# One PSUM ring for first scores and transposes, an earlier order of first scores, and sums and norms on GpSimd

## The chip, the cores and the metric

The kernel runs on one core of a Trainium2 chip. The metric is the device time of one execution in microseconds (us); lower is better. The engines of the core run side by side, each through its own list of instructions in order: TensorE (PE, with its weight loads PEld), VectorE (DVE), ScalarE (ACT), GpSimd (POOL) and SyncE (SP), which issues all DMAs of this kernel. TensorE writes its products to PSUM, here eight banks of 128 partitions by 512 fp32.

## The reference

A transformer block over 2048 rows of width 448, with an adaptive layer norm, sliding attention of 16 heads (28 wide, window 256) and a feed-forward part of width 1792:

```python
mod = (_silu(c) @ w_mod).reshape(c.shape[0], 6, 1, -1)
sa, ca, ga, sb, cb, gb = (mod[:, 0], mod[:, 1], mod[:, 2], mod[:, 3], mod[:, 4], mod[:, 5])
h = _layernorm(x, axis=-1) * (1 + ca) + sa
x = x + ga * _A_ref(h, A_wqkv, A_wo)      # softmax(q k^T, masked to the last 256 keys) v, then wo
h = _layernorm(x, axis=-1) * (1 + cb) + sb
x = x + gb * _B_ref(h, B_w1, B_b1, B_w2)  # mish(h w1 + b1) w2
return x
```

## The kernel before

The rows are cut into four groups of 512. Matrices are held as a rounded part and a rest (the tiles with h and l in their names), and a product is made of up to three passes, so that little accuracy is lost.

**Stages.** A prologue loads, makes the first two modulation vectors and the first group's q, k and v. Then comes the attention stage, the loop `for u in range(NU + 7)`, with NU = 192 units. After it, the feed-forward stage, which the change leaves alone.

**Heads, quads and units.** There are 64 heads i (16 in each of four groups, NS = 64). Four heads are a quad Q, and a quad has 12 units: unit u = 12 Q + 4 b + a is block b of head 4 Q + a. What one unit issues on TensorE is written out by hand in the loop.

- `A(i, t)` makes *first scores* for rows t of head i: one product of 384 columns into a bank of the tag sA (L687), and the rows' maximum by VectorE (L689). When a pair of heads is through, `M1` puts its eight maxima into a small tile `ms` (two VectorE steps).
- `M2(pr)` transposes the maxima of the pair pr on TensorE (L705), copies them by VectorE (L707) and writes them by a DMA into two more rows of the pair's q tiles. So the second scores come out with the maximum taken off.
- `B(u)` makes *second scores* in a bank sB0 or sB1 (L731; masks by TensorE, L759, or laid in by ScalarE, L739) and takes their exponential by ScalarE (L734).
- `PV(w)` multiplies four heads' exponentials with v (L769), `EV(q)` copies a quad's result to SBUF, `E(q)` transposes it on TensorE (L780), and `E2(q)` divides by the sums on VectorE (L788, L790).
- `L(i)`, called by `load_slot`, loads q and k of head i from DRAM into one of eight slots each. A slot is free when the second scores of head i - 8 have been made.

**Banks.** Before, the eight banks are sA two, mm two, sB0, sB1, pv and tr one each. `bank(tag, bufs, name)` takes the next of a tag's banks in a ring, and what writes it waits until the readers of its last content are through. The maxima's transposes and the outputs' transposes use tr.

**The order around the change.** In unit r of a quad (r = u mod 12), the first scores of the *next* quad stand at r = 1 to 10: score n (of 16) in unit 1 + 10 n // 16, the first of a unit right behind `B`, a second one at the unit's end; in unit 3 the first stands behind the filling work. `M2` stands at r = 7 and 11, the loads of a quad's four heads at units 8, 11, 14 and 16 counted from two quads before, and `E` and `E2` at r = 3 and 4 of the second quad behind.

**Filling work.** Between these, generators put other work in small steps: `fill_main` (transposes of the normed rows, q, k, v, the output product), taken by a credit of RATE per unit, and `side` (norms `gen_ln1`, weighted sums `gen_wm_sum`, weights), one step per unit. A step that yields "dve" is put off when the unit has two first scores. DMAs that a step needs later wait in the list `later`, from which the loop takes one in some of the units.

**Weighted sums and norms.** `gen_wm_sum(i)` loads four pieces of 112 rows of w_mod's column block i and adds them up, each scaled by a column of sT, with `mod_sum` (L167 for the first piece, L169 for the other three). It runs four times in the attention stage (i = 2, 3, 4, 5). Its result goes into a product on TensorE: L577 for i = 2, L174 for 3 and 4, L873 for 5. `gen_ln` norms four tiles of rows; L244 is the subtraction and scaling. It is used with the pool qk for the groups 2 and 3 before the attention of these groups, and with other pools later.

Of the kernel before, what the change touches and what calls it, by code (L numbers as in the profile page):

```python
# [12 lines left out]
ALU = mybir.AluOpType  # L13
# [38 lines left out]
def adaln_block(ctx: ExitStack, tc: tile.TileContext, x, wqkv, wo, w1, b1, w2, c, w_mod, out):  # L52
# [112 lines left out]
    def mod_sum(k, w, acc):  # L165
        if k == 0:
            DVE.tensor_scalar(acc, w, sT[:, 0:1], None, op0=ALU.mult)  # L167
        else:
            DVE.scalar_tensor_tensor(acc, w, sT[:, k:k + 1], acc, op0=ALU.mult, op1=ALU.add)  # L169
# [50 lines left out]
    def gen_ln(tiles, pl, xn_tiles, key, act=False, mv=None):  # L220
        if mv is None:
            mv = pl.tile([128, 4, 2], F32, name=f"mv{key}", tag="mv", bufs=2)
            for t in range(4):
                ln_stats(tiles[t], mv[:, t, :], pl, f"{key}{t}")
                if t < 3:
                    yield
        rs = pl.tile([128, 4], F32, name=f"rs{key}", tag="rs", bufs=2)
        POOL.tensor_scalar(rs, mv[:, :, 1], EPS, None, op0=ALU.add)
        POOL.tensor_tensor(rs, rs, mhalf, op=ALU.pow)
        yield  # L230
        if act:
            nm = pl.tile([128, 4], F32, name=f"nm{key}")
            POOL.tensor_tensor(nm, mv[:, :, 0], rs, op=ALU.mult)
            POOL.tensor_scalar(nm, nm, -1.0, None, op0=ALU.mult)
        yield
        xs = xn_tiles()
        for t in range(4):
            xn = xs[t]
            if act:
                ACT.activation(xn[:, 0:D], tiles[t], AF.Identity, scale=rs[:, t:t + 1], bias=nm[:, t:t + 1])  # L240
                dup(xn)
                yield xs
                continue
            DVE.tensor_scalar(xn[:, 0:D], tiles[t], mv[:, t, 0:1], rs[:, t:t + 1],  # L244
                              op0=ALU.subtract, op1=ALU.mult)
            if t:
                dup(xs[t - 1])
            yield xs
        if not act:
            dup(xs[3])  # L250
# [220 lines left out]
    pm = [bank("sA", 2, f"mc{h}") for h in range(2)]  # L471
# [28 lines left out]
    first = [(m, bank(tag, b, f"qk0_{m}"), qk_passes(0, m)) for m, tag, b in ((0, "pv", 1), (3, "tr", 1), (4, "sA", 2))]  # L500
# [72 lines left out]
    def gen_mod_wo():  # L573
        acc = yield from gen_wm_sum(2, qk)
        yield "bank"
        p = bank("mm", 2, "ga")
# [20 lines left out]
    def gen_mod_ln2(i):  # L597
        acc = yield from gen_wm_sum(i, qk)
        yield "bank"
        p = bank("mm", 2, f"mc{i}")  # L600
# [79 lines left out]
    def A(i, t):  # L680
# [5 lines left out]
        p = bank("mm" if i >= 60 and t % 2 else "sA", 2, f"sA{i}_{t}")  # L686
# [16 lines left out]
    def M2(pr):  # L703
        p = bank("tr", 1, f"mt{pr}")
# [72 lines left out]
    def E(q):  # L777
        p = bank("tr", 1, f"et{q}")
# [62 lines left out]
    def gen_w1():  # L841
# [19 lines left out]
        p = bank("mm", 2, "b1t")  # L861
# [10 lines left out]
        pb = bank("mm", 2, "gb")  # L872
# [235 lines left out]
    credit = 0.0  # L1108
    for u in range(NU + 7):
# [11 lines left out]
        q, r = divmod(u, 12)  # L1121
        if u < NU:
            B(u)
        tiles = [divmod(n, 4) for n in range(16) if 1 + n * 10 // 16 == r and 4 * q + 4 < NS]
        if r != 3:
            for a, t in tiles[:1]:
                A(4 * q + 4 + a, t)
        if r in (7, 11) and 4 * q + 4 < NS:
            M2(2 * q + 2 + (r == 11))
        for a in range(4):  # L1130
            if (u - (8, 11, 14, 16)[a]) % 12 == 0 and u >= (8, 11, 14, 16)[a]:
                load_slot(4 * ((u - (8, 11, 14, 16)[a]) // 12) + 8 + a)
        if r - 3 in (0, 1) and 0 <= (u - 12 - 3) // 12 < NS // 4:
            (E, E2)[r - 3](q - 1)
        if g < NG:
# [8 lines left out]
            if r == 3:  # L1144
                for a, t in tiles[:1]:
                    A(4 * q + 4 + a, t)
            if v > 1 and u > 10:
                side_step(g, len(tiles) > 1)
            if later and r in (1, 4, 5, 6, 8, 9) and u not in (4, 11, 12):
# [8 lines left out]
        for a, t in tiles[1:]:  # L1158
            A(4 * q + 4 + a, t)
# [98 lines left out]
```

## Time and profile before

| | us |
|---|---|
| median of 3 runs | 678.75 |
| lowest and highest | 676.63, 680.4 |
| span of the profiled execution | 674.8 |
| distance of the median from that span | 3.95 |

The profile is of one execution. A row of a group reads: line, engine, operation, out<-in, shape, xcount, then busy time and mean ns of one, then the idle time of the engine just ahead of them and what ended it. A row of a wait reads: who waited, at which line, for whom; total us, times, longest. A row of the timeline reads: start, length, engine, line, operation, and in brackets the idle time ahead of it. L59 is the helper that issues every DMA, so SP's rows are told apart by their tiles: q<-scr and k<-scr are the loads of `L`, q<-mr the maxima's rows of `M2`. PE's matmuls overlap, so the lengths shown for them add up to more than their starts allow.

### The profile page before, as it was taken

The page shows a single profiled execution, that of the slowest core. Times are in us where ns is not written, and L with a number is a line of the kernel's source. Part 1 is how long each engine was busy: PE and PEld are TensorE (multiplying, and loading weights), DVE is VectorE, ACT ScalarE, POOL GpSimd, SP SyncE. Part 2 cuts the span into 40 slices and gives each one's busy share as a digit, 9 for nine tenths or more (in the row PEclk, how much of TensorE's full clock was granted, in tenths as well). Part 3 has the DMA queues.
Part 4 walks back from the last instruction along what each step waited for, and adds up shares of the span by engine and source line. Part 5 has one row for each costly group of instructions (what it writes and reads, how often), then busy time and mean ns, then how long its engine had stood idle before and what let it go on. Part 6 is the DMA issues. An engine that isn't in the chain of part 4 may idle for free.

```text
span 674.8 us, 10729 instructions
## 1 busy us (share of the span) xinstructions
PE 637.9 (95%) x3712; PEld 511.0 (76%) x3712; DVE 391.7 (58%) x1138; ACT 336.9 (50%) x584; POOL 120.9 (18%) x173
## 2 busy tenths in 40 slices
PE   4998999899999999998989999989999999999996
PEld 3876676577887678776666788878888888888885
DVE  6865676756677767567767333963485438631112
ACT  4554566678765677734667743442333323322221
POOL 6741010233011100000030245431012001100002
PEclk9999999999999999997999999999999999999999
DMA  8875775456855478434772654003000300010001
GB/s 227 225 234 191 263 260 159 134 149 197 279 138 156 140 220 289 144 107 113 192 217 63 220 162 137 14 1 110 0 1 0 109 2 0 1 54 1 1 0 54
DMA packets 49169, 83.77 MB, mean 124 GB/s; under 512 B 5838, under 2 KB 27612, under 8 KB 49116
## 3 DMA queue, kind: packets, MB, share of 16 engines
q1 hardware_dynamic: 49116, 83.10, 40.3%
q8 instruction: 29, 0.48, 0.3%
q14 instruction: 24, 0.20, 0.1%
HBM read 53.45 MB, written 29.36 MB: 123 GB/s over the span
## 4 chain that ended last, share of the span: by engine, by line
PE 66%; DVE 15%; issue 12%; DMA 3%; ACT 2%; POOL 1%; SPq 0%; POOLq 0%; DVEq 0%; ACTq 0%
PE z L970 15%; PE qk L321 8%; DVE junk L689 6%; PE sA L687 6%; PE pv L769 6%; PE sB L731 5%; PE acc L1179 4%; PE acc L1178 4%; PE acc L1177 4%; PE wo L321 3%; PE qk_v L321 3%; DVE yt L897 3%; PE sB L759 2%; DMA k<-scr 1%; PE qk L506 1%
## 5 line engine op out<-in xcount | busy, mean ns | idle before, releaser
L689 DVE CUSTOM_DVE_ANT_0 junk<-sA,strip 128x384 bf16<-128x384 f32 (+2 forms) x256 | 135.7, 530 | 91.6 <-PE sA L687 76.7
L734 ACT ACTIVATE P<-sB 128x512 f32<-128x512 f32 (+2 forms) x192 | 108.6, 571 | 99.1 <-PE sB L731 96.7
L978 DVE TENSOR_TENSOR al<-t,ah 128x512 fp32r<-128x512 f32 x56 | 41.2, 736 | 137.2 <-ACT ah L977 136.8
L976 ACT ACTIVATE t<-z,b1c 128x512 f32<-128x512 f32 x56 | 38.4, 686 | 156.8 <-PE z L970 145.8
L687 PE MATMUL sA<-k,q 84*128 84x384 f32 (+2 forms) x256 | 93.5, 370 | 10.7 <-DVE mx L689 6.2
L970 PE MATMUL z<-hhf,w 128*128 128x512 f32 x224 | 89.0, 397 | 0.0
L970 PE MATMUL z<-hlf,w 128*128 128x512 f32 x224 | 88.8, 396 | 0.0
L731 PE MATMUL sB<-q,k 86*128 86x384 f32 (+1 forms) x352 | 84.9, 316 | 0.0
L1179 PE MATMUL acc<-w2h,al 128*128 128x448 f32 x224 | 82.1, 366 | 1.9 <-DVE al L978 1.9
L1177 PE MATMUL acc<-w2h,ah 128*128 128x448 f32 x224 | 81.9, 366 | 0.0
L1178 PE MATMUL acc<-w2l,ah 128*128 128x448 f32 x224 | 81.8, 365 | 0.0
L731 PEld LDWEIGHTS sB<-q,k 86*128 86x128 f32 x352 | 59.4, 193 | 13.1 <-issue 5.1
L970 PE MATMUL z<-hhf,w1l 128*128 128x512 f32 x168 | 66.5, 396 | 0.0
L687 PEld LDWEIGHTS sA<-k,q 84*128 84x128 f32 x256 | 48.3, 191 | 23.2 <-DVE mx L689 15.1
L897 DVE STREAM_TRANSPOSE yt<-xn 32x128 f32<-32x128 f32 x192 | 58.1, 302 | 2.6
L739 ACT ACTIVATE sB<-strip 128x512 f32<-128x512 bf16 (+2 forms) x95 | 54.6, 575 | 3.0
L769 PE MATMUL pv<-P,v 128*32 128x256 f32 (+2 forms) x704 | 50.6, 402 | 0.0
L970 PEld LDWEIGHTS z<-hlf,w 128*128 128x128 f32 x224 | 42.1, 188 | 10.1
L970 PEld LDWEIGHTS z<-hhf,w 128*128 128x128 f32 x224 | 42.1, 188 | 9.1 <-issue 0.6
L1179 PEld LDWEIGHTS acc<-w2h,al 128*128 128x128 f32 x224 | 42.1, 188 | 5.9 <-DVE al L978 2.6
L1177 PEld LDWEIGHTS acc<-w2h,ah 128*128 128x128 f32 x224 | 42.1, 188 | 5.0
L1178 PEld LDWEIGHTS acc<-w2l,ah 128*128 128x128 f32 x224 | 42.1, 188 | 4.8
(155 smaller groups left out, 1024.2 us busy)
## 6 DMA issues: line engine op xcount, KB each, us to landing
k<-scr SPq DMA_DIRECT2D x48, 252.0 KB
q<-scr SPq DMA_DIRECT2D x64, 168.0 KB
scr<-st SPq DMA_DIRECT2D x21, 512.0 KB
scr<-st SPq DMA_DIRECT2D x29, 256.0 KB
x<-x1d SPq DMA_DIRECT2D x10, 448.0 KB
xin<-in_A_x_dram SPq DMA_DIRECT2D x8, 448.0 KB
xr<-in_A_x_dram SPq DMA_DIRECT2D x16, 224.0 KB
x1d<-xr SPq DMA_DIRECT2D x16, 224.0 KB
```

Of the source, the lines that this page charges most:

```text
L321: PE.matmul(p, b, a, start=(n == 0), stop=(n == 10))
L687: PE.matmul(p[:, c0:384], q[0:84, t * 128:(t + 1) * 128], k[0:84, t * 128 + c0:t * 128 + 384], start=True, stop=True)
L689: DVE.tensor_tensor_reduce(out=junk[:, c0:384], in0=p[:, c0:384], in1=mask[:, c0:384], scale=1.0, scalar=-3.0e38, op0=ALU.add, op1=ALU.max ...
L731: PE.matmul(p[:, c:c + 128 * (t1 - t0)], k[:, jj * 128:(jj + 1) * 128], q[:, t0 * 128:t1 * 128], start=False, stop=True, skip_group_check= ...
L734: ACT.activation(P[:, c0:], p[:, c0:], AF.Exp, scale=SCALE)
L739: ACT.activation(p[:, c0:], strip[:, c + c0:c + 512], AF.Copy)
L769: PE.matmul(pvb[q][32 * a:32 * a + 32, t0 * 128:t1 * 128], V[j % NV][:, h + a, :], Pt[4 * w + a][:, c:c + 128 * (t1 - t0)], start=(b == 0 ...
L897: DVE.transpose(y4[32 * j:32 * j + 32, ci, :, 32 * i:32 * i + 32], x4[32 * i:32 * i + 32, :, ci, 32 * j:32 * j + 32])
L970: PE.matmul(zb[n], ps[m][1], ps[m][0], start=(m == 0), stop=(m == 10))
L1177: PE.matmul(p, ah[n][:, ts], w2h[f], start=(f == 0), stop=False)
L1178: PE.matmul(p, ah[n][:, ts], w2l[f], start=False, stop=False)
L1179: PE.matmul(p, al[n][:, ts], w2h[f], start=False, stop=(f == NF - 1))
```

## The change

There are four parts.

1. **Banks.** The tag tr goes away and sA gets a third bank. The maxima's transposes (`M2`), the outputs' transposes (`E`), and the small products of the modulation vectors and of b1 (L577, L174, L873, L862), which used tr or mm, take their banks from the ring sA. The last heads' first scores, which took turns between sA and mm, use sA alone.
2. **Order.** The tables `scores`, `maxima`, `slots` and `outs` are made ahead of the loop. With u0 = 12 (Q - 1), score n of quad Q now stands in unit u0 - 1 + 11 n // 16, the first of a unit always right behind `B`; `M2` at u0 + 5 and u0 + 11; the loads at 8, 10, 12 and 15 counted from two quads before; `E` and `E2` together at 12 Q + 16. The units that take from `later` are 1, 2, 4, 6, 7 and 9 in place of 1, 4, 5, 6, 8 and 9.
3. **Weighted sums.** `mod_sum` runs on GpSimd: a scaling of each piece and, for three of the four, an add.
4. **Norms.** L244 runs on GpSimd where the pool is qk, that is for the groups 2 and 3: eight instructions.

```diff
     def mod_sum(k, w, acc):
-        if k == 0:
-            DVE.tensor_scalar(acc, w, sT[:, 0:1], None, op0=ALU.mult)
-        else:
-            DVE.scalar_tensor_tensor(acc, w, sT[:, k:k + 1], acc, op0=ALU.mult, op1=ALU.add)
+        POOL.tensor_scalar(w, w, sT[:, k:k + 1], None, op0=ALU.mult)
+        if k:
+            POOL.tensor_tensor(acc, w, acc, op=ALU.add)
...
-            DVE.tensor_scalar(xn[:, 0:D], tiles[t], mv[:, t, 0:1], rs[:, t:t + 1],
-                              op0=ALU.subtract, op1=ALU.mult)
+            (POOL if pl is qk else DVE).tensor_scalar(xn[:, 0:D], tiles[t], mv[:, t, 0:1], rs[:, t:t + 1],
+                                                      op0=ALU.subtract, op1=ALU.mult)
...
-        p = bank("mm" if i >= 60 and t % 2 else "sA", 2, f"sA{i}_{t}")
+        p = bank("sA", 3, f"sA{i}_{t}")
...
     def M2(pr):
-        p = bank("tr", 1, f"mt{pr}")
+        p = bank("sA", 3, f"mt{pr}")
...
     def E(q):
-        p = bank("tr", 1, f"et{q}")
+        p = bank("sA", 3, f"et{q}")
...
+    scores, maxima, slots, outs = {}, {}, {}, {}
+    for Q in range(1, NS // 4):
+        u0 = 12 * (Q - 1)
+        for n in range(16):
+            scores.setdefault(max(u0 - 1 + n * 11 // 16, 0), []).append((4 * Q + n // 4, n % 4))
+        maxima[u0 + 5], maxima[u0 + 11] = 2 * Q, 2 * Q + 1
+    for i in range(8, NS):
+        slots[12 * (i // 4 - 2) + (8, 10, 12, 15)[i % 4]] = i
+    for Q in range(NS // 4):
+        outs[12 * Q + 16] = Q
...
-        tiles = [divmod(n, 4) for n in range(16) if 1 + n * 10 // 16 == r and 4 * q + 4 < NS]
-        if r != 3:
-            for a, t in tiles[:1]:
-                A(4 * q + 4 + a, t)
-        if r in (7, 11) and 4 * q + 4 < NS:
-            M2(2 * q + 2 + (r == 11))
-        for a in range(4):
-            if (u - (8, 11, 14, 16)[a]) % 12 == 0 and u >= (8, 11, 14, 16)[a]:
-                load_slot(4 * ((u - (8, 11, 14, 16)[a]) // 12) + 8 + a)
-        if r - 3 in (0, 1) and 0 <= (u - 12 - 3) // 12 < NS // 4:
-            (E, E2)[r - 3](q - 1)
+        tiles = scores.get(u, [])
+        for a, t in tiles[:1]:
+            A(a, t)
+        if u in maxima:
+            M2(maxima[u])
+        if u in slots:
+            load_slot(slots[u])
+        if u in outs:
+            E(outs[u])
+            E2(outs[u])
...
-            if later and r in (1, 4, 5, 6, 8, 9) and u not in (4, 11, 12):
+            if later and u % 12 in (1, 2, 4, 6, 7, 9) and u not in (4, 11, 12):
                 later.pop(0)()
```

The other lines of the diff give the banks of the small products and of the prologue the tag sA with three banks.

More of the change, by code (lines that the diff above doesn't have):

```diff
@@ L470, in adaln_block @@
         dup(XS[0][t])
-    pm = [bank("sA", 2, f"mc{h}") for h in range(2)]
+    pm = [bank("sA", 3, f"mc{h}") for h in range(2)]
     trs = [bank(*((f"sB{ci}", 1) if ci < 2 else ("mm", 2)), f"tr0{ci}") for ci in range(4)]
@@ L499, in adaln_block @@
         wq_lo(0, ci, POOL)
-    first = [(m, bank(tag, b, f"qk0_{m}"), qk_passes(0, m)) for m, tag, b in ((0, "pv", 1), (3, "tr", 1), (4, "sA", 2))]
+    first = [(m, bank(tag, b, f"qk0_{m}"), qk_passes(0, m)) for m, tag, b in ((0, "pv", 1), (3, "sA", 3), (4, "sA", 3))]
     def passes0(cs, half):
@@ L575, in gen_mod_wo @@
         yield "bank"
-        p = bank("mm", 2, "ga")
+        p = bank("sA", 3, "ga")
         PE.matmul(p[:, 0:D], ones, acc, start=True, stop=True)
@@ L599, in gen_mod_ln2 @@
         yield "bank"
-        p = bank("mm", 2, f"mc{i}")
+        p = bank("sA", 3, f"mc{i}")
         mod_cols(acc, p)
@@ L860, in gen_w1 @@
         b1c = FW["b1c"] = p1.tile([128, NF], F32, name="b1c")
-        p = bank("mm", 2, "b1t")
+        p = bank("sA", 3, "b1t")
         PE.transpose(p[:, 0:NF], b1r, ident[0:NF, 0:NF])
@@ L871, in gen_w1 @@
         yield "bank"
-        pb = bank("mm", 2, "gb")
+        pb = bank("sA", 3, "gb")
         PE.matmul(pb[:, 0:D], ones, acc, start=True, stop=True)
@@ L1143, in adaln_block @@
                 credit -= step(g)
-            if r == 3:
-                for a, t in tiles[:1]:
-                    A(4 * q + 4 + a, t)
             if v > 1 and u > 10:
                 side_step(g, len(tiles) > 1)
-            if later and r in (1, 4, 5, 6, 8, 9) and u not in (4, 11, 12):
+            if later and u % 12 in (1, 2, 4, 6, 7, 9) and u not in (4, 11, 12):
                 later.pop(0)()
@@ L1158, in adaln_block @@
         for a, t in tiles[1:]:
-            A(4 * q + 4 + a, t)
+            A(a, t)
     for st in (FW["s2"], att_s, vp_s):
```

1 line of the change is left out of this document (removed).

## The prediction

> **What bounds the kernel now.** I read the page's first part, then the busy time by stretch (the attention stage from 40 to 372 us, the feed-forward stage behind it), then the waits of the attention stage.
>
> ```profile
> span 674.8 us, 10729 instructions
> PE 637.9 (95%) x3712; PEld 511.0 (76%) x3712; DVE 391.7 (58%) x1138; ACT 336.9 (50%) x584; POOL 120.9 (18%) x173
> ```
>
> ```profile
> 40.00:372.00 332.00, 314.15 (x2202) 233.68 (x2201) 226.59 (x760) 217.28 (x394) 38.17 (x50) 0.98 0.59 181
> 372.00:668.00 296.00, 294.12 (x1376) 252.91 (x1374) 136.81 (x320) 101.03 (x159) 52.17 (x55) 1.00 0.15 46
> ```
>
> The columns of a stretch are its length, then the busy time of PE, PEld, DVE, ACT and POOL, the granted clock, the DMA share and GB/s. Behind 372 us PE idles for 2 of 296 us, and the change touches nothing there. In the attention stage PE idles for 17.85 of 332 us. That is the most that is visible to win, so the waits behind it come next.
>
> ```profile
> PEld sA L687 <- DVE mx L689: 15.1, 34, 1.6
> ...
> PEld mt L705 <- DVE ms L701: 9.9, 15, 1.9
> PE mt L705 <- DVE ms L701: 6.6, 11, 1.7
> PE sA L687 <- DVE mx L689: 6.2, 21, 1.4
> PE sA L687 <- DMA k<-scr: 2.0, 2, 1.1
> ```
>
> Each row gives the total, the times and the longest wait. Two waits on DVE stand out: a first score (L687) that needs its bank back from the maximum (L689), and the maxima's transpose (L705) that needs the last DVE step of a pair (L701). The weight load (PEld) and the matmul (PE) show different sizes of the same wait. Single instructions tell which is nearer:
>
> ```profile
> 114.10 0.44 PE L687 MATMUL sA<-k,q 84*128 84x384 f32 x1 [0.15 <-DVE mx L689]
> ...
> 114.81 0.19 PEld L687 LDWEIGHTS sA<-k,q 84*128 84x128 f32 x1 [0.52 <-DVE mx L689]
> 114.81 0.44 PE L687 MATMUL sA<-k,q 84*128 84x384 f32 x1 [0.27 <-DVE mx L689]
> ...
> 121.19 0.56 PE L687 MATMUL sA<-k,q 84*128 84x384 f32 x2
> ```
>
> Two scores that wait start 0.71 us apart (114.81 less 114.10). Two that don't wait take 0.56 us together, though each is shown as about 0.39 to 0.44 long, so the second starts at most some 0.17 us after the first. The loss is about 0.54 us, which is PEld's 0.52 and not PE's 0.27. So the PEld rows are near the true price: 15.1 and 9.9 us, with 6.2 and 6.6 as lower ends.
>
> **The third bank and DVE's relief.** A first score now waits for the maximum three places back in the ring instead of two. What one place is worth, and what DVE gives away:
>
> ```profile
> L689 DVE CUSTOM_DVE_ANT_0 junk<-sA,strip 128x384 bf16<-128x384 f32 x253 | 134.4, 531 | 88.1 <-PE sA L687 73.2 <-PE sB L731 0.5
> L689 DVE DVE_READ_ACCUMULATOR2_ANT mx<- 128x1 f32 x254 | 21.0, 83 | 0.0
> ...
> L169 DVE SCALAR_TENSOR_TENSOR wm<-wm,sT,wm 112x448 f32<-112x448 f32 x12 | 8.1, 673 | 0.1
> ...
> L244 DVE TENSOR_SCALAR xin<-xin,mva,rsa 128x448 f32<-128x448 f32 x8 | 4.1, 507 | 0.0
> ...
> L167 DVE TENSOR_SCALAR wm<-wm,sT 112x448 f32<-112x448 f32 x4 | 1.8, 445 | 0.0
> ```
>
> One place is one maximum, 531 + 83 = 614 ns. The 34 waits of 15.1 us are 0.44 us long in the mean, so most would end. DVE also loses 8.1 + 4.1 + 1.8 = 14.0 of its 226.6 busy us. Against this, 32 maxima's transposes, 16 outputs' transposes and 5 small products now take places in the same ring, so some 309 places are taken instead of 256. And where scores come one behind the other, as at 114 us, the 0.71 us is DVE's own rate for a score, which no bank changes. Bounds: nothing to 15.1 us. I take 9 us, three fifths, with the 14.0 us of relief inside it: it is what lets DVE catch up between the dense places.
>
> **The maxima's transposes.** Before, the second pair of a quad has its last score in unit 10 and its transpose in unit 11, the next. After, the last score is in unit 9, the transpose still in unit 11.
>
> ```profile
> 124.06 0.28 PE L705 MATMUL mt<-ident,ms 128*16 128x128 f32 x1 [0.96 <-DVE ms L701]
> ...
> L707 DVE COPY mr<-mt 16x128 f32<-16x128 f32 x32 | 8.8, 274 | 3.3 <-PE mt L705 3.3
> ```
>
> This 0.96 us is such a wait; one more unit, some 1.5 us (a third of the way from 102.04 to 106.49 in the rows below), covers it. The two pairs of the prologue keep their place, and one of these is the longest wait, 1.9. Their bank now comes from the ring and goes back after the 274 ns copy, for which a score may wait. Bounds: nothing to 9.9 less 1.9. I take 6 us gone. What is late next on PE is then the score itself, or the data that it reads.
>
> **The scores further ahead: their loads.** A quad's first score moves two units ahead, but the load of its q and k can't: the slot's last reader is the second score of eight heads before.
>
> ```profile
> 102.91 0.37 SPq L59 DMA_DIRECT2D q<-scr  x1
> 103.33 0.37 SPq L59 DMA_DIRECT2D k<-scr  x1
> 107.78 0.62 SPq L59 DMA_DIRECT2D q<-mr  x1
> 108.50 0.36 SPq L59 DMA_DIRECT2D q<-scr  x1
> ```
>
> ```profile
> 102.04 0.40 PE L731 MATMUL sB<-q,k 86*128 86x384 f32 x2
> ...
> 106.49 0.40 PE L731 MATMUL sB<-q,k 86*128 86x384 f32 x2
> ...
> 110.34 0.34 PE L687 MATMUL sA<-k,q 84*128 84x384 f32 x1
> ```
>
> For head 16 the last reader ends at 102.4, the loads go out at 102.91 and 103.33, and the first score starts at 110.34. Five units lie between. In the new order it stands behind the unit of 106.49, three units after the reader, so at 106.9: 3.6 us after k's issue. How long such a load takes when something waits for it:
>
> ```profile
> 33.38 4.12 DMA k<-scr
> ...
> 125.96 4.92 DMA k<-scr
> ```
>
> ```profile
> 269.46 0.34 SPq L59 DMA_DIRECT2D q<-scr  x1
> ```
>
> ```profile
> 274.89 0.41 PE L731 MATMUL sB<-q,k 86*128 86x384 f32 x2
> ```
>
> With 4.1 to 4.9 us it lands 0.5 to 1.3 us late there. In the later groups units are longer: for head 48, q goes out at 269.46, k some 0.4 later, and the third unit ends at 275.3, which is 5.4 us after k's issue and in time by 0.5 to 1.3. So of 14 quads the three or four of the first group are late by about 0.9 us, 3.5 us, and the others by little unless a store is ahead in the queue; stores are now taken up in units 6 and 7 in place of 5 and 6, nearer to the load of unit 8. I add 1.5 us for that. On the other side, the load of the quad's second head leaves SP's queue only behind the maxima's row (107.78, then 108.50), and in the new order it goes out ahead of it. That can remove the 2.0 us of waits for k above. Net: 3 us lost; bounds 2 gained, to 14 x 1.3 = 18 lost.
>
> **The work that moves to GpSimd.** Sixteen scalings and twelve adds replace the sums, and eight norms come with them.
>
> ```profile
> L590 POOL TENSOR_TENSOR wop<-wop,ga 128x448 f32<-128x448 f32 x4 | 4.6, 1152 | 0.0
> ...
> L218 POOL COPY xin<-xin 128x64 f32<-128x64 f32 x11 | 2.6, 237 | 35.6 <-DVE xin L244 26.1 <-PE sA L687 4.9 <-ACT xin L240 3.8
> ...
> L792 POOL COPY on<-on 128x256 f32<-128x256 f32 x3 | 1.2, 397 | 90.6 <-DVE on L790 90.6
> ```
>
> An add is 1.15 us by L590. A scaling of 448 columns isn't in the trace; from copies of 64 and 256 columns (0.24 and 0.40) the line goes to 0.56 us, and 1.15 is the upper end. I take 0.56, since a scaling has one large input as a copy has. POOL gains 16 x 0.56 + 12 x 1.15 + 8 x 0.56 = 27 us on its 38 in this stage, which fits into 332. What counts is the end of each chain, where PE has a product of the sums in its order:
>
> ```profile
> 129.12 1.27 POOL L302 TENSOR_TENSOR hl<-y,hh 128x512 fp32r<-128x512 f32 x1 [1.03 <-ACT hh L258]
> ...
> 131.94 0.68 DVE L169 SCALAR_TENSOR_TENSOR wm<-wm,sT,wm 112x448 f32<-112x448 f32 x1
> ...
> 134.00 0.92 PE L577 MATMUL ga<-wm,ones 112*128 112x448 f32 x2
> ```
>
> The last sum starts 2.06 us before the product. On POOL it takes 0.56 + 1.15 = 1.71 us, which just fits, or 2.3 with the dearer scaling; another 1.27 us if a split (L302) is ahead of it. Over four chains: nothing to 4 us. I take 1. Behind a waiting product stand the scores and all else on PE.
>
> [...]
>
> **What comes back, and the sum.**
>
> ```profile
> ACT P L734 <- PE sB L731: 96.7, 105, 5.2
> ```
>
> ACT idles 96.7 us for second scores, so it takes a closer order of PE mostly without a wait; I leave 1 us for dense places. The sum: 9 + 6 less 3, 1 and 1 = 10 us. The span goes from 674.8 to about 665. What lies around the span of the profiled execution isn't shown for it; the median of the three runs is 678.75, which is 3.95 above the span. With the same distance the forecast is 678.75 less 10 = 668.8 us.
>
> **Rivals.** *The loads take the place of the waits (slower).* The mechanism is the three units from reader to score. It decides by how late the load lands: at 15 / 14 = 1.1 us per quad it eats both gains. If stores make every load take 6 us instead of 4.9, the late ones cost about 1.4 us in each of 14 quads, 20 us: 678.75 less 15, plus 20, plus 2 = 686. For it: the 4.92 us above, and lead that shrinks from 7.0 to 3.6 us. Against: the later units are longer. 0.11.
>
> *The banks change nothing, because DVE's rate bounds (no change).* Then the score's wait stays and moves, and of the maxima's 6 us the loads eat 3 and the rest 2: some 678. For it: 0.71 us a score in a row at 114 us. Against: DVE is busy for 226.6 of 332 us. 0.14.
>
> *GpSimd is late.* Each of the four products waits for about 2 us, the norms hold up nothing since their transposes come much later: 668.8 plus 6 = 675. For it: the 2.06 us. Against: POOL is busy for 38 of 332 us. 0.09.
>
> *All waits go.* 15.1 + 8 + 2 and no late loads: 678.75 less 24 = 655. 0.06. The forecast's own case has the remaining 0.60, 662 to 674.
>
> **How the numbers follow.** A measurement of this kernel can tell about 0.5%, 3.4 us, from no change. Faster by more: 0.60 + 0.06 and the 0.09 of late GpSimd at 675 (just beyond 3.4): 0.75. Within: 0.14. Slower: 0.11. The range that leaves out the slower rival and part of the case in which all waits go is 659 to 679.
>
> **What would show it.** Right: the two PEld rows at under 7 and under 4 us, PE idle in the attention stage down from 17.85 us, a row of PE waiting for k or q of 2 to 6 us, and the same 296 us behind it. Wrong: waits of PE for DMA over 12 us, waits of L577, L174 or L873 for POOL, or the score's wait as long as before. The forecast fails most easily at the load of unit 8.

## The result and the profile after

| | us |
|---|---|
| changed kernel, median of 4 runs | 689.12 (685.68 to 690.56) |
| kernel before, median of 4 runs beside it | 677.69 (676.54 to 680.4) |
| ratio, with 95% interval | 1.0163 [1.0126, 1.0199] |
| span of the profiled execution after (its own time 689.51) | 687.4 |

The changed kernel is 1.6% slower. The forecast was 668.8 us, the range 659 to 679. Ratios here and below are of the usual executions alone: of the ten of one run (first scores one unit ahead), three at 683.7 to 685.7 us are counted as slow and left out of its ratio, though not of its median. The first part of the page after:

```profile
span 687.4 us, 10733 instructions
PE 642.1 (93%) x3712; PEld 516.3 (75%) x3712; DVE 382.6 (56%) x1114; ACT 337.6 (49%) x584; POOL 170.5 (25%) x209
```

The work went where the change sends it: DVE has 9 us less, POOL 50 more. PE's 4 us more of busy time is no new work (3712 matmuls in both); it is largely the same work at a lower clock, as will be seen. By stretches, the attention stage, the passage to the feed-forward stage, and that stage:

```profile
40.00:382.00 342.00, 318.69 (x2211) 239.95 (x2210) 218.56 (x741) 219.61 (x396) 88.35 (x88) 0.97 0.58 177
382.00:392.00 10.00, 8.02 (x53) 5.79 (x52) 3.60 (x7) 8.44 (x14) 0.00 (x0) 1.00 0.66 200
392.00:680.00 288.00, 285.69 (x1320) 247.00 (x1321) 132.59 (x313) 92.64 (x145) 51.47 (x55) 1.00 0.13 41
```

In the attention stage PE now idles for 23.3 of 342 us, where it was 17.85 of 332. From 392 us on all is as before; in the 10 us between, PE idles for 2, in a wait that comes up again below. The waits of the attention stage after, first PE's, then the weight loads' (total, times, longest):

```profile
PE sA L686 <- DMA k<-scr: 15.6, 11, 3.8
PE mt L704 <- DVE ms L700: 2.3, 1, 2.3
```

```profile
PEld sA L686 <- DVE ms L700: 5.1, 3, 2.1
...
PEld sA L686 <- DVE mx L688: 3.9, 8, 1.8
PEld mt L704 <- DVE ms L700: 2.9, 3, 2.5
...
PEld sA L686 <- DVE ms L699: 1.8, 1, 1.8
```

Read this against the two rows of before. The first score's wait for the maximum fell from 15.1 to 3.9 us, though some of it came back as waits for a pair's other DVE steps (5.1 and 1.8), which stand in the same order. The transpose's wait fell from 9.9 to 2.9. In their place stands one row that was 2.0 us: first scores wait 15.6 us for k. The chain that ended last shows the same; each row is its start, its length and what it is:

```profile
81.53 6.25 DMA k<-scr
...
258.33 5.24 DMA k<-scr
```

In ten places from 81 us on the end of the kernel hangs on a load of k, from its issue to its landing. The worst is head 44. Its place: SP's queue in the timeline (start, length, instruction), then the slot's last reader in the chain, then the late score in PE's timeline:

```profile
250.78 0.63 SPq L59 DMA_DIRECT2D q<-mr  x1
251.51 0.35 SPq L59 DMA_DIRECT2D wm<-in_w_mod_dram  x1
251.99 3.18 SPq L59 DMA_DIRECT2D scr<-st  x4
255.27 0.86 SPq L59 DMA_DIRECT2D wm<-in_w_mod_dram  x1
256.23 0.94 SPq L59 DMA_DIRECT2D scr<-st  x2
257.26 1.01 SPq L59 DMA_DIRECT2D q<-scr  x1
258.33 0.65 SPq L59 DMA_DIRECT2D k<-scr  x1
```

```profile
253.82 0.23 PE sB L730 x2
```

```profile
263.71 0.41 PE L686 MATMUL sA<-k,q 84*128 84x384 f32 x1 [3.77 <-DMA k<-scr]
```

The slot was free at 254.05 (253.82 + 0.23). But a maxima's row, two loads of w_mod and six stores stood ahead in SP's queue, and SP, which goes through its list in order, had first waited for DVE's copy of that row:

```profile
SPq L59 <- DVE mr L706: 6.3, 1, 6.3
```

So all that stood behind the row went out late and in one bunch, the load of head 44 last. Its q went out at 257.26 and its k at 258.33; 5.24 us later k was there, and PE had stood still for 3.77 us.

Which heads were late can be counted along SP's queue. Of the 15.6 us, 8.1 are waits for the first heads of a quad (16, 20, 24, 28 and 44). The other 7.5 are for heads of the second pair (11, 18, 54, 58, 59 and 62). For these the change left four units between load and score, as before, and their slots had been free for two or four units when the load was issued.

Now the place of head 44 by stretches (length, busy PE, PEld, DVE, ACT, POOL, granted clock, DMA share, GB/s):

```profile
254.00:264.00 10.00, 6.23 (x43) 4.49 (x42) 2.50 (x9) 5.76 (x11) 5.07 (x4) 1.00 0.86 251
264.00:270.00 6.00, 6.00 (x35) 4.00 (x34) 2.96 (x10) 2.96 (x6) 0.00 (x0) 0.72 0.51 142
270.00:276.00 6.00, 6.00 (x45) 4.76 (x43) 4.63 (x16) 4.55 (x9) 0.00 (x0) 1.00 0.99 364
```

Behind the gap the clock is 0.72 for 6 us, and PE, busy throughout, gets through 35 matmuls where the next 6 us hold 45. So this wait is paid a second time. Over the whole span the granted clock was 0.990 before and is 0.981 after. (1 - 0.990) x 674.8 = 6.7 us and (1 - 0.981) x 687.4 = 13.1 us are an estimate of the time that the lower clock stands for, as if PE had been busy throughout: 6.4 us more.

One wait is new in the feed-forward stage's head, where before there was none:

```profile
L1181 PE MATMUL acc<-w2h,ah 128*128 128x448 f32 x224 | 82.0, 366 | 2.4 <-DVE on L789 2.4
```

The outputs' transposes now hold a bank of the shared ring, and the first bank of the feed-forward sum waits for its division (L789).

These terms nearly give the difference of the spans, 12.6 us: waits for k +13.7 (16.4 with the prologue's, from 2.7), clock +6.4, the bank +2.4, first scores' waits for DVE -4.3 (15.1 to 3.9 + 5.1 + 1.8), transposes -7.0; together 11.2. This is a bookkeeping of one execution each, with smaller rows left out, and not yet a proof. The experiments follow.

### The profile page after: what moved, and what is told of

Read it like the earlier page. It is cut to its first block, busy times and chain, and to the rows that moved or that the text cites. A ratio compares the mean times of both kernels' runs of the same rounds, so it can differ in the third digit from the quotient of the medians.

```text
span 687.4 us, 10733 instructions
## 1 busy us (share of the span) xinstructions
PE 642.1 (93%) x3712; PEld 516.3 (75%) x3712; DVE 382.6 (56%) x1114; ACT 337.6 (49%) x584; POOL 170.5 (25%) x209
## 3 DMA queue, kind: packets, MB, share of 16 engines
HBM read 53.45 MB, written 29.36 MB: 120 GB/s over the span
## 4 chain that ended last, share of the span: by engine, by line
PE 66%; issue 11%; DMA 9%; DVE 8%; ACT 3%; SPq 1%; POOL 1%; POOLq 0%; DVEq 0%; ACTq 0%
PE z L969 14%; DMA k<-scr 8%; PE qk L320 8%; PE sA L686 6%; PE pv L768 5%; PE sB L730 5%; PE wo L320 4%; PE acc L1183 4%; PE acc L1181 4%; PE acc L1182 4%; PE qk_v L320 3%; DVE yt L896 3%; PE sB L758 2%; DVE junk L688 2%; PE qk L505 1%
## 5 line engine op out<-in xcount | busy, mean ns | idle before, releaser
L733 ACT ACTIVATE P<-sB 128x512 f32<-128x512 f32 (+2 forms) x192 | 108.5, 570 | 90.4 <-PE sB L730 88.8
L686 PE MATMUL sA<-k,q 84*128 84x384 f32 (+2 forms) x256 | 93.1, 371 | 17.6 <-DMA k<-scr 16.4
```

The source lines that it names most:

```text
L686: PE.matmul(p[:, c0:384], q[0:84, t * 128:(t + 1) * 128], k[0:84, t * 128 + c0:t * 128 + 384], start=True, stop=True)
L733: ACT.activation(P[:, c0:], p[:, c0:], AF.Exp, scale=SCALE)
```

## The experiments

Each ratio is to the kernel before, run beside it (its medians there lay between 676.6 and 678.9 us), with its 95% interval. Line numbers in an edited kernel can differ by one or two.

**Which part loses the time.** Five runs take parts alone or undo one.

The changed kernel, first scores put back to the old units:

```diff
-            scores.setdefault(max(u0 - 1 + n * 11 // 16, 0), []).append((4 * Q + n // 4, n % 4))
-        maxima[u0 + 5], maxima[u0 + 11] = 2 * Q, 2 * Q + 1
+            scores.setdefault(u0 + 1 + n * 10 // 16, []).append((4 * Q + n // 4, n % 4))
+        maxima[u0 + 7], maxima[u0 + 11] = 2 * Q, 2 * Q + 1
```

> The changed kernel with first scores and the maxima's transposes in the units they had before (score n at 1 + 10 n // 16, transposes at 7 and 11); ring of three banks, loads' new units, sums and norms on GpSimd stay. Theory A, the two units of lead starve the first scores of k and q (16.4 us of waits for k in the changed kernel against 2.7 before) and each long wait is followed by a stretch at a lower granted clock: the waits for k fall under 4 us, the mean granted clock goes back to about 0.99, and the time falls from 689 to about 670. Theory B, GpSimd's slow sums and norms (1.40 and 1.86 us an instruction) hold SP's queue and the products: the time stays over 683. Theory C, the one ring of three banks for scores, maxima and outputs is what costs: it stays over 683, with waits of first scores for DVE.

Measured: 682.57 us, 1.0078 [1.0047, 1.011]. Waits of PE for k are 2.9 us, as theory A said, but the time is 12 us above its 670, and the clock of the profiled span is 0.979, no higher than the 0.981 of the changed kernel. So the late loads are not all of it: without the lead the clock is low in other places (the last section shows one).

The changed kernel with sums and norms back on DVE:

```diff
-        POOL.tensor_scalar(w, w, sT[:, k:k + 1], None, op0=ALU.mult)
-        if k:
-            POOL.tensor_tensor(acc, w, acc, op=ALU.add)
+        if k == 0:
+            DVE.tensor_scalar(acc, w, sT[:, 0:1], None, op0=ALU.mult)
+        else:
+            DVE.scalar_tensor_tensor(acc, w, sT[:, k:k + 1], acc, op0=ALU.mult, op1=ALU.add)
...
-            (POOL if pl is qk else DVE).tensor_scalar(xn[:, 0:D], tiles[t], mv[:, t, 0:1], rs[:, t:t + 1],
+            DVE.tensor_scalar(xn[:, 0:D], tiles[t], mv[:, t, 0:1], rs[:, t:t + 1],
```

> The changed kernel with the weighted sums and the two norms back on VectorE; all else as changed. Theory A (lead): still slow, 684 to 689, with over 12 us of waits for k. Theory B (GpSimd holds SP's queue, and with it the loads): 674 to 679, the wait for head 44's k of 3.8 us gone and the waits for k under 8 us. Theory C (ring): 686 to 692, since VectorE gets 14 us more work and all DVE waits grow.

Measured: 693.83 us, 1.0239 [1.0194, 1.0283], above what each theory said. The waits in its profile:

```profile
PE sA L687 <- DMA k<-scr: 18.5, 13, 4.0
```

The late loads are there without GpSimd, so the move to GpSimd is not what makes the kernel slow; in this company it rather helps, by some 5 us, but between two runs whose intervals overlap a little.

The kernel before with the third bank and the shared ring alone, in the old order:

```diff
-        p = bank("mm" if i >= 60 and t % 2 else "sA", 2, f"sA{i}_{t}")
+        p = bank("sA", 3, f"sA{i}_{t}")
...
-        p = bank("tr", 1, f"mt{pr}")
+        p = bank("sA", 3, f"mt{pr}")
```

> The kernel before with the ring of three banks alone: scores, maxima's and outputs' transposes and the small products in sA, everything else as before. Theory A and B: faster than before by 5 to 10 us (668 to 673), since the 15.1 us that weight loads of first scores waited for DVE fall by half or more. Theory C: slower than before, 680 to 688, with new waits of transposes for the ring.

Measured: 675.63 us, 0.9977 [0.9954, 1.0000]. Its weight loads' waits:

```profile
PEld sA L687 <- DVE mx L689: 9.6, 23, 1.3
...
PEld mt L705 <- DVE mx L689: 4.3, 10, 0.7
```

The third bank takes 5.5 us from the first row. The last row is new: the transposes, which had a bank of their own, now wait 4.3 us for a score's bank. What is left, 1.2 us, is about the 1.6 us (0.23%) measured, where theories A and B had said 5 to 10.

The kernel before with sums and norms on GpSimd alone, and then with banks and GpSimd together, in the old order:

```diff
+        POOL.tensor_scalar(w, w, sT[:, k:k + 1], None, op0=ALU.mult)
+        if k:
+            POOL.tensor_tensor(acc, w, acc, op=ALU.add)
```

> The kernel before with the weighted sums and the two norms on GpSimd, and nothing else changed. Theory A (loads late through lead and SP's order; GpSimd's relief of VectorE is a gain): 672 to 676, since VectorE loses 14 us and the first scores' waits for it fall. Theory B (GpSimd's slow instructions, 1.40 and 1.86 us, hold products and buffers): 679 to 683.

> The kernel before with the ring of three banks and the sums and norms on GpSimd; scores, transposes, loads and stores in their old units. It stands against the kernel with the lead undone (682.6), which differs from it by the loads' units, the outputs' units and the units that take stores. Theory A: 671 to 675, so that those three units' tables cost some 8 to 10 us. Theory B: near 682, so that GpSimd is what the lead-undone kernel loses by.

Measured: 678.88 us, 1.0024 [1.0001, 1.0048], and 676.93 us, 1.0003 [0.9976, 1.0031]. DVE's relief buys nothing by itself; the theories that took it for a gain had said 672 to 676 and 671 to 675.

**How much lead, and which units for the stores.** The changed kernel with first scores only one unit further ahead than before:

```diff
-            scores.setdefault(max(u0 - 1 + n * 11 // 16, 0), []).append((4 * Q + n // 4, n % 4))
-        maxima[u0 + 5], maxima[u0 + 11] = 2 * Q, 2 * Q + 1
+            scores.setdefault(u0 + n * 10 // 16, []).append((4 * Q + n // 4, n % 4))
+        maxima[u0 + 6], maxima[u0 + 11] = 2 * Q, 2 * Q + 1
```

> The changed kernel with one unit of lead in place of two (score n at u0 + 10 n // 16, transposes at u0 + 6 and u0 + 11). Theory A: between the kernel with no lead and the changed one, 674 to 682, with 4 to 10 us of waits for k. Theory B and C: within 2 us of the changed kernel.

Measured: 680.94 us, 1.0015 [0.9979, 1.005], between the two, as theory A said, with 7.0 us of PE's waits for k.

The store list in its old units, without the lead and with it:

```diff
-            if later and u % 12 in (1, 2, 4, 6, 7, 9) and u not in (4, 11, 12):
+            if later and u % 12 in (1, 4, 5, 6, 8, 9) and u not in (4, 11, 12):
```

> The kernel with the lead undone, and the stores taken up in units 1, 4, 5, 6, 8 and 9 as before. What is left of the changed order are the loads' units and the outputs' units. Theory A1, stores taken up in units 6 and 7 stand ahead of the maxima's rows and the loads in SP's queue: 674 to 678, and the 2.2 us wait of second scores for the maxima's rows goes. Theory A2, the loads' or outputs' own units cost: 680 to 684.

> The changed kernel with the stores taken up in units 1, 4, 5, 6, 8 and 9 as before. Theory A1: 680 to 685, and head 44's load goes out within 1 us of its slot's release (3.2 us in the changed kernel), with its 3.8 us wait gone. Theory A2: 687 to 690.

Measured: without the lead 680.46 us, 1.0026 [0.9992, 1.006]; with it 690.59 us, 1.0215 [1.0155, 1.0276], and its profile has the row of after nearly unchanged:

```profile
PE sA L686 <- DMA k<-scr: 16.5, 9, 4.2
```

With the lead undone the old units of the stores are 0.5% faster, with the lead 0.5% slower, and neither is clear of the intervals; so the stores' units are not what the changed kernel loses by. The lead is: everything else being equal, it costs 1.9% with the old units of the stores (1.0215 against 1.0026) and 0.8% with the new ones (1.0163 against 1.0078). The 0.8% that the kernel with the lead undone is still slower than before was not taken apart further.

**What the late loads cost.** These two leave out the loads of q and k from head 8 on (the slots keep the first heads' data, the K slots are filled whole at the start), once in the changed kernel and once with the lead undone:

```diff
+        if i >= 8:
+            return
```

> The changed kernel without the loads of q and k from head 8 on: second and first scores read what the slots hold (slots are filled whole with -1 at the start), so no first score can wait for a load and SP's queue has 112 DMAs less. Theory A (the loads, late for the earlier scores, are what costs): 668 to 675, that is 14 us or more below the changed kernel. Theory D (the earlier order of scores itself costs, by VectorE or the banks, and the waits for k only stand where other waits would): over 682.

> The kernel with the lead undone, without the same loads. Against the one above it gives the worth of the two units of lead when loads cost nothing. Theory A: 674 to 678, so the lead is worth 3 us or more with loads out of the way. Theory D: 672 to 678 and faster than the one above by 4 us or more.

Measured: 664.86 us, 0.9826 [0.9774, 0.9879], and 679.36 us, 0.9995 [0.997, 1.002]. The first one's span and clock:

```profile
core 0: 661.0 us, clock 0.996
```

With loads that are never late the lead is worth 2.1% of 679.36 us, and the changed kernel without them is 1.7% faster than the kernel before. Against the changed kernel's span 26.4 us are gone: 15.6 of waits for k (0.8 is left) and (1 - 0.981) x 687.4 less (1 - 0.996) x 661.0 = 10.4 of clock, 26.0 together. A limit of this test: it also takes HBM reads from 53.45 to 30.06 MB, so other transfers may have had more room. But the second run has the same room, and it gains only 3.2 us by it (682.57 to 679.36), where the first gains 24.3 (689.12 to 664.86). So the loads cost much only in company with the lead.

**Whether a gap really costs more than itself.** Two runs start from the banks-alone kernel (span 673.9 us, clock 0.987) and put six known gaps into PE's order, in units 67, 79, 91, 103, 115 and 127: a tiny product, a scaling on GpSimd that waits for it, and a tiny product that waits for the scaling.

```diff
+        if u in (67, 79, 91, 103, 115, 127):
+            p = bank("sA", 3, f"zz{u}")
+            PE.matmul(p[:, 0:1], zz[:, 0:128], ones[:, 0:1], start=True, stop=True, skip_group_check=True)
+            for _ in range(1):
+                POOL.tensor_scalar(zz[:, 0:256], zz[:, 0:256], 0.5, None, op0=ALU.mult)
+            PE.matmul(p[:, 1:2], zz[:, 0:128], ones[:, 0:1], start=True, stop=True, skip_group_check=True)
```

> The kernel before with the ring of three banks, and in six units (67, 79, 91, 103, 115, 127) a tiny product that waits for a GpSimd scaling of 112 x 256, which itself waits for a tiny product ahead of it: TensorE stands still for about 1.1 us each time. Theory E (a stall over some 1.5 us is followed by a stretch at half the granted clock, a shorter one isn't): 6 x 1.1 to 1.3 us over the banks alone, 682 to 684, no stretch of lower clock behind any of the six. Theory F (lower clock comes on its own, not from stalls): the same.

The second has two scalings of all 448 columns in each place:

```diff
-            for _ in range(1):
-                POOL.tensor_scalar(zz[:, 0:256], zz[:, 0:256], 0.5, None, op0=ALU.mult)
+            for _ in range(2):
+                POOL.tensor_scalar(zz[:, 0:448], zz[:, 0:448], 0.5, None, op0=ALU.mult)
```

> The same six stalls with two scalings of 112 x 448 each, so about 3 us each time. Theory E: a stretch of 5 to 7 us at half the clock behind most of the six, and some 6 x (3 + 3) = 36 us over the banks alone, 705 to 715. Theory F: 6 x 3 = 18 us, 692 to 696, with no more low stretches than in the kernel with short stalls.

Measured: 692.82 us, 1.0214 [1.0175, 1.0252], and 716.67 us, 1.0553 [1.0519, 1.0587]. The wait in each:

```profile
PE zz L1131 <- POOL zz L1130: 8.0, 6, 2.6
```

```profile
PE zz L1131 <- POOL zz L1130: 19.4, 6, 4.5
```

The spans grew by 18.0 us (to 691.9) for 8.0 us of gaps, and by 41.4 (to 715.3) for 19.4: 2.1 to 2.3 us for each us that PE stands still. One of the six long gaps by stretches:

```profile
188.00:191.40 3.40, 0.47 (x5) 0.38 (x3) 0.85 (x4) 1.95 (x4) 2.66 (x2) 0.90 0.71 274
191.40:197.00 5.60, 5.58 (x17) 5.06 (x18) 1.37 (x6) 0.48 (x1) 0.00 (x0) 0.50 0.03 12
197.00:203.00 6.00, 6.00 (x45) 4.83 (x44) 4.00 (x15) 4.22 (x9) 0.00 (x0) 0.95 0.20 72
```

PE does 17 matmuls in the 5.6 us behind the gap and 45 in the 6 us after those. All six long gaps have such a stretch; of the six short ones only the 2.6 us and one of 1.1 us do. The clock of the long run is 0.955: (1 - 0.955) x 715.3 less (1 - 0.987) x 673.9 = 23.4, and with the gaps 42.8, which is the 41.4 measured. For the short run the same sum gives 6.5 + 8.0 = 14.5 of 18.0; 3.5 us stay unexplained (each place also takes a bank of the ring), and both theories had said 682 to 684. The long run is near theory E, which had said 705 to 715, and far from F.

**Why the loads are late, and whether they needn't be.** The slot of a quad's first head comes free three units before its next use, and SP's queue holds other things then. Four runs move the loads ahead in the order and the stores to other units, with the full lead, with a lead of one unit, and each with one more filling step ahead of the prologue's second transpose:

```diff
-        slots[12 * (i // 4 - 2) + (8, 10, 12, 15)[i % 4]] = i
+        slots[12 * (i // 4 - 2) + (8, 9, 10, 11)[i % 4]] = i
...
-        if u in maxima:
-            M2(maxima[u])
         if u in slots:
             load_slot(slots[u])
+        if u in maxima:
+            M2(maxima[u])
...
-            if later and u % 12 in (1, 2, 4, 6, 7, 9) and u not in (4, 11, 12):
+            if later and u % 12 in (0, 1, 2, 3, 4, 11) and u not in (4, 11, 12):
```

> The changed kernel with its first scores as far ahead as they are there, but the loads of a quad's four heads in units 8, 9, 10 and 11 (the changed kernel: 8, 10, 12, 15), each ahead of the maxima's row of the same unit, and the stores taken from their list in units 0, 1, 2, 3, 4 and 11 (there 1, 2, 4, 6, 7, 9), so that SP has nothing left ahead of a quad's first load. Theory 'order': the loads were late because of what stood ahead of them in SP's queue; with them in front, PE's waits for k fall from 16.4 us to under 5, the half-clock stretches behind them go, and the time comes near the 664.9 us of the run without loads: 668 to 675. Theory 'lifetime': the first head of a quad frees its slot only three units before its next use, and no order helps: the waits of heads 12, 16, 20, 28 stay, those of 44, 18, 54, 58, 59 and 62 go, k waits 6 to 10 us, 676 to 684.

> The same order of loads and stores, with first scores only one unit further ahead than before (n-th tile of a quad in unit 10n/16, maxima in 6 and 11), so that a quad's first head has four units between its slot's last reader and its first score. Theory 'order': nothing more to be had beyond the run with the full lead; less lead brings more waits for DVE, so 2 to 5 us above it. Theory 'lifetime': a unit more takes away what the order leaves: k waits under 3 us, and 668 to 676, below both kernels and below the run with the full lead.

The step in the prologue:

```diff
-            fill0((1, 1, 1, 0)[i])
+            fill0(1 if i < 3 or t == 3 else 0)
```

> As the first of these four, with one step of the filling work between the last first score of the prologue and the second transpose of maxima, which waited 2.3 us in the changed kernel and was followed by a stretch at half clock from 52 to 62 us. Theory 'gap lowers the clock': the stretch goes and with it some 3 to 4 us against the first of these runs. Theory 'the clock falls there for other reasons' (few matmuls in flight while scores are dense): the stretch stays, and the time is within 1 us of it.

> The second of these four with the same step in the prologue. Theory 'gap lowers the clock': 3 to 4 us below the second run. Theory 'other reasons': within 1 us of it. If 'lifetime' and 'gap lowers the clock' both hold, this is the fastest of all, 665 to 673 us, below the kernel before.

Measured: 706.92 us, 1.045 [1.0419, 1.0482]; 714.42 us, 1.0559 [1.0537, 1.0581]; 706.3 us, 1.0437 [1.0398, 1.0476]; 715.77 us, 1.057 [1.053, 1.0611]. All four are slower than every theory said. PE's waits in the first:

```profile
PE sA L686 <- DMA k<-scr: 10.2, 4, 4.4
...
PE sB L730 <- DMA q<-mr: 7.7, 4, 3.1
```

The loads gained 6 us, but the maxima's rows, for which the changed kernel shows no such wait, cost 7.7. (The weight loads show 6.3 us for them too; these are two of the same four moments and don't add.) One more wait is new, and it comes from the stores' units: a tile `st` was still held by its store (the chain that ended last has a store of `st` there, 5.21 us long from 177.48).

```profile
PE qk_v L320 <- DVE st L349: 4.4, 1, 4.4
```

Nor did the edit clear SP's queue where it mattered most. For head 44 the slot was free at 264.12, and its q went out at 266.51, behind a row, a load of w_mod and six stores as in the changed kernel; PE waited 3.74 us. The waits of heads 16, 20 and 28, which theory 'lifetime' said would stay, went. So both theories were wrong, and 'order' was not put to a clean test.

With the lead of one unit PE's waits for k fall to 1.0 us (its weight loads show one more of 3.5), and the rows' grow:

```profile
PE sB L730 <- DMA q<-mr: 16.7, 6, 5.3
```

The rows are late for two reasons. Of the 7.7 us with the full lead, 3.1 and 2.8 are for two rows that were ready 4.3 and 3.6 us before SP issued them, since the stores and the loads now ahead of them held the queue. The first one, its copy by DVE and then SP's queue:

```profile
73.35 0.27 DVE L706 COPY mr<-mt 16x128 f32<-16x128 f32 x1
```

```profile
72.41 3.32 SPq L59 DMA_DIRECT2D scr<-st  x4
75.83 1.18 SPq L59 DMA_DIRECT2D q<-scr  x1
...
77.92 0.63 SPq L59 DMA_DIRECT2D q<-mr  x1
```

And a row, which is 8 KB, takes longer to land behind several heads' loads. In the changed kernel most rows land 1.9 to 2.0 us after their issue; here the one that PE waited 1.6 us for took 5.1:

```profile
344.61 5.10 DMA q<-mr
```

About the prologue the two pairs say little. Its gap went from 2.27 to 1.57 us, and the times moved by -0.6 and +1.4 us, not by the 3 to 4 that 'gap lowers the clock' had said. But with the full lead no half-clock stretch had followed the gap of 2.27 us, and with the lead of one unit a stretch followed both the gap of 2.27 us and that of 1.57.

Last, the rows from GpSimd's queue instead of SP's, with the loads ahead as above, with the full lead and with a lead of one:

```diff
-        dma(Q2[pr % (NQ // 2)][84:86].bitcast(F32).rearrange("i a (t n) -> i (a t) n", t=4), r)
+        POOL.dma_start(Q2[pr % (NQ // 2)][84:86].bitcast(F32).rearrange("i a (t n) -> i (a t) n", t=4), r)
```

> The run with the loads ahead and the full lead (706.9 us), with one thing more: the maxima's rows are issued from GpSimd's queue instead of SP's, so that rows and loads no longer stand ahead of one another. Theory 'one queue': in that run the rows were what came late (PE and its weight loads waited 14 us for q from the row, in gaps of 1.6 to 4.4 us with half-clock stretches behind them); on a queue of their own those waits go, and what is left is the 10 us of waits for k: 672 to 684. Theory 'lifetime' adds that the first heads' loads (20, 44, 60) stay late, 1.6 to 4.4 us each, so that the time lies in the upper half of that. Rival 'GpSimd's queue is no better': a row waits there behind scalings of 1.4 us and norms of 1.9 us and costs GpSimd time of its own; row waits stay over 8 us, and it takes 690 to 705.

> The run with the loads ahead and a lead of one unit (714.4 us; waits for k 4.5 us, for rows over 23 us), with the rows from GpSimd's queue. Theory 'one queue': both waits are gone, and it is the fastest of all, 665 to 675, below the kernel before. Rival 'GpSimd's queue is no better': 690 to 712.

Measured: 729.26 us, 1.0779 [1.0744, 1.0813], and 726.83 us, 1.0724 [1.0685, 1.0764], slower than even the rival said. From the first one's waits and groups:

```profile
PE sB L730 <- DMA q<-mr: 31.6, 12, 4.0
...
PE sA L686 <- DMA k<-scr: 2.7, 2, 1.4
```

Here the loads are on time with the full lead: 2.7 us, as in the kernel before. So with the rows out of SP's queue the loads can be on time, which speaks for SP's order, rows included, as what made most of them late. It is no proof: units are longer in so slow a run (its span is 728.1 us), and that gives the loads more time too. And the rows are now late by 31.6 us on PE. GpSimd's queue is mostly not why: for 28 of the 32 rows GpSimd issued the row 0.3 to 0.4 us after DVE's copy had ended. What is long is the way from issue to landing, for all rows and for the one behind PE's longest wait:

```profile
DMA to landing us min/median/max: 1.8/3.4/7.4
```

```profile
118.17 7.43 DMA q<-mr
```

Where four or more loads of q and k (168 and 252 KB each) had gone out in the 5 us before a row, it landed after 3.8 to 7.4 us; of the other 18 rows all but two landed within 3.1. So the rival was right that GpSimd's queue is no better, but for a reason that it didn't name: in these runs a small transfer lands late behind big ones, though another engine issues it. No run has both on time. The best time of all with nothing left out is that of the banks alone, 675.63 us, which its interval does not tell from no change.

## Why the prediction was wrong, step by step

From the forecast span of about 665 us to the measured 687.4 it is 22.4 us. The bookkeeping above places 21.2 of them: waits for k 10.7 more than the 3 allowed, the clock 6.4, first scores 4.7 less gained than the 9 taken, the new wait in the feed-forward stage 2.4, less 1 us more gained at the transposes and 2 us taken for GpSimd and ACT that no row shows.

- **The loads of q and k** (net 3 us lost; bounds 2 gained, 18 lost) is the step that failed. The mechanism was named rightly, three units from the reader to the score, and so was the place, the load of unit 8. Its size was off twice. Waits for k grew by 13.7 us instead of 3, since the step took the issue for prompt: it priced SP's queue with 1.5 us, while head 44 alone lost 3.2 us there. For the early quads it was nearly right: it gave them 3.5 us, and heads 16, 20, 24 and 28 were late by 4.3 together. The rest is head 44's 3.8 us and 7.5 us for heads of the second pair, which the step did not look at. And the sum had no term at all for the clock: the trace of before already had a stretch at 0.53, behind a gap of 1.36 us (its row stands at the end of this section), and it wasn't read. Without late loads 26.4 us of the span are gone, 10.4 of them clock. Stores ahead in the queue, which the step named as what would make it worse, did make it so at head 44; but the stores' old units did not help (1.0215).
- **The third bank and DVE's relief** (9 us). By itself the bank is worth 1.6 us, and together with DVE's relief nothing that can be told (1.0003). The 53 places that transposes and products take in the ring were counted but not priced; the transposes' new wait, 4.3 us, was most of the missing gain. In the changed kernel the first row fell to 3.9 us, under the 7 that would show the step right, but that was mostly the lead's doing: with the lead undone it is 7.1.
- **The maxima's transposes** (6 us). Right: 7.0 us gone, and only the prologue's wait is left, 2.3 us. That one grew from 1.7, where the prologue's last four scores now run in a row.
- **GpSimd** (1 us lost). Right in effect, wrong in size: the scaling was taken at 0.56 us with 1.15 as the upper end and took 1.40, a norm 1.86. No product of L576, L173 or L872 shows up among PE's larger waits for POOL, and undoing the move made the changed kernel no faster (1.0239 against 1.0163).
- **ACT** (1 us). ACT's own wait for second scores went from 96.7 to 88.8 us; nothing shows a loss.
- **What the sum left out**: the first feed-forward bank behind the outputs' division, 2.4 us. The prediction said that the change touches nothing there. The row stands in every profile with the full lead and in none with the lead undone or of the banks alone; why was not taken apart.
- **The rivals.** What happened is the first, the loads in place of the waits: 686 us at a chance of 0.11, measured 689.1. That the number is so near is partly luck, since its reason, every load taking 6 us in each of 14 quads, is not how it went: 11 first scores waited, the ten loads in the chain took 3.8 to 6.3 us, and the clock did the rest. "All waits go", 655 us, is nearest to the run without loads, 664.9, and still 10 us below it.

The stretch of before that should have been read (columns as above; 36 matmuls in 7 us of busy time):

```profile
306.00:313.00 7.00, 6.73 (x36) 4.68 (x36) 4.70 (x15) 1.79 (x3) 0.40 (x1) 0.53 0.85 216
```

The gap of 1.36 us ahead of it, in PE's timeline of before:

```profile
305.98 0.44 PE L687 MATMUL sA<-k,q 84*128 84x384 f32 x1 [1.36 <-DVE mx L689]
```

Of the changed kernel's late loads head 44's, 3.77 us, is the longest; low clock stands behind waits much shorter than that too, and with the six gaps of 2.9 to 4.5 us each us cost 2.1.

## What to carry to other kernels

Issuing consumers earlier is worth only as much as their inputs can be earlier too (here 1.7% faster without the loads, 1.6% slower with them): before moving a step ahead, list for each input when its buffer comes free, what stands ahead of its load in the queue, which issue in that queue waits for a step that is not done yet, and when small urgent transfers would land behind big ones (here rows of 8 KB took 3.8 to 7.4 us behind four or more loads in one run, against 1.9 to 2.0 for most in the changed kernel). In this kernel gaps of 3 to 4.5 us on TensorE cost about twice their length (41.4 us for 19.4), and six of 1.1 to 2.6 us cost 18.0 us for 8.0, with low clock behind two of them; a stretch of low granted clock in the trace of before is a reason to give the clock a term of its own. A bank added to a ring pays only when what else joins the ring is paid for (here 5.5 us less of one wait, 4.3 us of a new one).

## What the runs showed of the hardware

Half clock follows a gap, but not each time. The granted clock falls to 0.50 for 3.4 us to at least 9 at all six gaps of 2.9 to 4.5 us, and at gaps of 1.58, 1.64 and 1.90 us in the changed kernel. Gaps of 1.26, 1.30, 1.33 and 1.39 us there did nothing, and neither did one of 2.40 at the head of the feed-forward stage. In the kernel before, a gap of 1.69 us did nothing, and half clock followed one of 1.36 and, 1.6 us after its end, one of 1.05.

The same prologue gap of 2.27 us stands in the profiles of 14 runs: in ten of them half clock begins within 2 us of its end, in four it doesn't. It does in the changed kernel (the first two rows) and doesn't in the run with the loads ahead (the last two):

```profile
52.00:56.00 4.00, 2.04 (x8) 1.78 (x9) 2.27 (x9) 0.83 (x2) 1.58 (x2) 0.69 0.19 67
56.00:60.00 4.00, 4.00 (x18) 3.46 (x17) 1.87 (x8) 1.12 (x2) 0.00 (x0) 0.50 0.68 214
```

```profile
52.00:56.00 4.00, 1.68 (x11) 1.27 (x10) 2.84 (x13) 1.69 (x3) 2.42 (x2) 1.00 0.34 102
56.00:60.00 4.00, 3.14 (x23) 2.42 (x22) 2.30 (x10) 2.44 (x5) 0.42 (x1) 1.00 0.49 158
```

In the kernels before and after, each stretch of half clock is 3.4 or 6.8 us long, but for the last of each, which runs into the end of the span; in other runs there are stretches of 10.2 us too. Why the same gap acts in one run and not in another was not shown.

There is also half clock with no gap over 1.3 us: with the lead undone and no loads the clock was 0.975 over the whole span of the profiled execution (up to 0.988 in others), and from 121 to 131 us PE was at half clock. In the 2 us from 120 PE was idle for 1.28 in all, in the 2 us before those for 0.02.

```profile
120.00:124.00 4.00, 2.72 (x14) 1.43 (x13) 3.33 (x13) 1.26 (x3) 0.26 (x1) 0.65 0.00 1
124.00:128.00 4.00, 3.51 (x17) 2.81 (x13) 2.04 (x8) 1.81 (x4) 0.00 (x0) 0.50 0.01 3
```

From 120 to 124 us DVE was busy for 3.33 of 4 us and PE for 2.72; that PE ran densely placed first scores at DVE's rate there is the author's reading. A stretch of the same 10.2 us, beginning between 119 and 122 us, stands in the profiles of seven other runs that leave the first scores in the old units, though not in that of the kernel before. Most of what the lead is worth without loads is in the clock: the spans of the two runs without loads differ by 16.8 us, and their clocks stand for (1 - 0.975) x 677.8 less (1 - 0.996) x 661.0 = 14.3 of it. Whether many small gaps set this off was not tried.

On GpSimd a scaling with one large input took longer here than an add with two:

```profile
L166 POOL TENSOR_SCALAR wm<-wm,sT 112x448 f32<-112x448 f32 x16 | 22.4, 1403 | 28.3 <-DMA wm<-in_w_mod_dram 28.3
...
L243 POOL TENSOR_SCALAR xin<-xin,mva,rsa 128x448 f32<-128x448 f32 x8 | 14.9, 1861 | 0.2
L168 POOL TENSOR_TENSOR wm<-wm,wm 112x448 f32<-112x448 f32 x12 | 13.6, 1136 | 1.0
```

The scaling takes 1.40 us, the norm with two scalars 1.86, the add 1.14; on DVE the first two took 0.45 and 0.51.
